# Loading ScalarE's sigmoid table first, spreading batch 1's folds one a step, and reordering the loads and the first products of a Fourier mixing and gated feed-forward kernel

## The chip, the cores and the metric

The kernel runs on one core of one Trainium2 chip. A core has a matrix engine (TensorE, PE in the profile, with its weight loads as PEld), a vector engine (VectorE, DVE), a scalar engine (ScalarE, ACT), a general engine (GpSimd, POOL), and SyncE (SP), which only issues DMAs here. Transfers run on 16 DMA engines that all queues share. SP, ACT and POOL each issue DMAs; the instructions of an engine, DMA issues among them, go in their order.

The metric is the device time in microseconds (us). The kernel before takes 1187.11 us, the median of three runs (1185.74 to 1187.33).

## The reference

```python
def _attn_ref(x):                        # x: 8 x 3136 x 256
    X = np.fft.fft(x, axis=1)
    X = np.fft.fft(X, axis=2)
    return X.real.astype(np.float32)

def _moe_ref(x, w_in, conv_w, w_out):    # 256 x 1024, 3 x 1024, 1024 x 256
    h = np.maximum(x @ w_in, 0.0)
    ...                                  # a zero row ahead of and behind h gives hp
    for k in range(3):
        conv_out += conv_w[k][None, None, :] * hp[:, k:k + S, :]
    gate = 1.0 / (1.0 + np.exp(-conv_out))
    return (h * gate @ w_out).astype(np.float32)
```

The second function is applied to the result of the first. The three weights arrive as 64-bit floats, `x` as 32-bit.

## The kernel before, in words

**Transform along the sequence.** For each of the 8 batches the kernel folds `x` by the symmetries of the transform. Two halves of `x` (`load_ops(b, 0, ...)` and `load_ops(b, 1, ...)`) come in, each as one plain load on SP and four mirrored gathers issued by POOL. `fold_ops(b)` gives eight operations for each half: two pair sums (`pair`), a difference and a sum (`both`), the odd features (`feats(1)`), `turned`, `evens`, and the even features (`feats(0)`). They are DVE work, with small POOL copies (`single`) and ScalarE scalings (`scaled`) beside them. For batch 0 `scaled` makes scaled copies (tiles `h`, called `parted`) and `turned` does nothing; for the other batches `turned` combines in place what `scaled` made.

`units(b)` then multiplies the folded rows by tables of cosines and sines. A unit is a group of matmuls, a copy on ScalarE and a finishing (`fin`) on DVE. There are four odd units (they use `tabs[1]`, the odd tables, of which half is mirrored by `mirror_tables` on ScalarE after `mend_row(1, ...)` halved one row) and four even ones (`tabs[0]`), and for batch 0 a small unit for one feature row. The finishings write the two matrices `qt` and `pt` (`PQ[b]`), 128 features x 1569 frequencies.

**Transform along the features, joined with w_in.** `blocks(i)` multiplies `dm`, the features' matrix, by a quarter of `w_in` and gives a quarter of `G`; `column(i)` gives one column of it, `ge`. `w_in` is narrowed from 64 to 32 bits by `narrow`: seven DVE operations, or, where a `room` is given, five on DVE and one on ScalarE. `taps` prepares the three convolution weights `cw`: one matmul, one ScalarE copy and six small DVE operations.

**The main loop.** A step is a batch, one of 4 chunks of frequencies, and one of 8 blocks of 128 of the 1024 hidden features: 256 steps, 32 a batch. `products` multiplies `G` with `qt` (PSUM tile `pb`) and with `pt` (`pa`, seeded by `seed`); `copies` takes `pb` out on ScalarE; `combine` adds both with a ReLU on DVE; `first_tap`, `middle` (an accumulating DMA) and `last_tap` are the convolution; `sigmoid` and `gate` follow four steps later; `mm2` multiplies by `w_out` five steps later and stores.

**What sets the order.** It is written out by hand. Ahead of the loop the program order is each engine's order: loads; the narrowing of the first weights and `taps`; all folds of batch 0; filler matmuls (`keep_on`) on PE while nothing else is ready; the odd units in four parts each (`part(i)`; parts 0 and 1 use x's first half, parts 2 and 3 its second); the feature unit and the even units; `column(0)`, `blocks(0)` and the narrowing of `w_in[1]`. In the loop, a table `side[(cycle, where)]` puts everything else at a step and at a place within the step: the narrowing of weights ("first" and "dve", steps 0 to 10), the folds and units of the next batch ("dve", "act", "pool", "pe"), and the loads ("load"). `ends[b]` is the step at which batch b's units begin; the folds of batch b lie between `ends[b-1]` and `ends[b]`, for batch 1 at the steps of a list.

Memsets of single elements by POOL (L118, L720 to L722) make the loads that write the same tile wait until POOL has issued its gathers. Lines that matter below: L157 to L228 folds, L261 to L280 tables, L288 `turn` (the factors of `scaled`), L296 and L302 mending and mirroring, L355 to L418 finishings, L619 to L637 narrowing, L698 to L706 `taps`, L740 and L750 copies of `G` and `ge`, L788 `copies`, L796 `combine`, L811 `last_tap`, L826 `sigmoid`, L835 `gate`. All matmuls have line L93, so PE's rows are told apart by their tiles.

## Time and profile before

| | us |
|---|---|
| median of the runs | 1187.11 (1185.74 to 1187.33) |
| profiled execution, its own time | 1188.7 |
| its span, first to last instruction | 1186.9 |
| busy: PE, DVE, ACT, POOL | 1144.0, 963.0, 945.9, 594.2 |
| PE weight loads | 890.8 |

The busy time is the time in which an engine had an instruction under way. A row of a timeline gives start, length, engine, line, operation, the tile written, the tiles read, shapes, how many instructions were merged, and in square brackets the idle time ahead of them on that engine with what ended it. A matmul of 32-bit floats stands as two instructions. A row of the groups gives the count, then busy us and mean ns of one, then idle us ahead with their releasers. An engine name with a q behind it is that engine's DMA issue.

### The profile page before, as it was taken

To read this page: it belongs to the slowest core of one execution; us is meant where nothing else is said; L and a number is where in the kernel's file an instruction comes from. 1 tells how busy PE (TensorE), PEld (TensorE's weight loads), DVE (VectorE), ACT (ScalarE), POOL (GpSimd) and SP (SyncE) were. 2 spreads that over 40 slices of the span, in tenths; PEclk is the share of its full clock that TensorE was granted. 3 is DMA by queue.
4 is the path that set the end of the run, shared out by engine and by line. 5 is a ranking of instruction groups with operands and counts; after the bars stand their busy time and mean duration, and the time that the engine had idled before them with its cause. 6 is when DMAs were issued, how large, how long until landed. Compare 5 with 4: busy or idle time off the path is not lost.

```text
span 1186.9 us, 16040 instructions
## 1 busy us (share of the span) xinstructions
PE 1144.0 (96%) x4818; PEld 890.8 (75%) x4818; DVE 963.0 (81%) x1448; ACT 945.9 (80%) x1939; POOL 594.2 (50%) x734
## 2 busy tenths in 40 slices
PE   4988999999999999999999999999999999999998
PEld 2755777777777787777777777777778777777777
DVE  7589988887888888988885887889788677788885
ACT  2488778787887888888887888888787788898884
POOL 5244745655374454556455464654444444444443
PEclk9899999999999999999999999999999999999999
DMA  8666696785677676867675576756565556666664
GB/s 206 191 99 145 152 166 147 156 174 119 136 170 160 129 157 143 169 134 170 143 162 131 94 175 143 170 128 130 117 125 117 115 122 139 131 134 124 129 119 98
DMA packets 107586, 168.15 MB, mean 142 GB/s; under 512 B 32657, under 2 KB 62627, under 8 KB 107501
## 3 DMA queue, kind: packets, MB, share of 16 engines
q0 software_dynamic: 41984, 115.83, 50.9%
q1 hardware_dynamic: 64345, 50.89, 15.1%
q8 instruction: 38, 0.62, 0.2%
q10 hardware_dynamic: 1172, 0.43, 0.2%
q14 instruction: 47, 0.39, 0.1%
HBM read 38.40 MB, written 25.74 MB: 54 GB/s over the span
## 4 chain that ended last, share of the span: by engine, by line
PE 70%; ACT 7%; DVE 6%; issue 3%; DMA 2%; POOL 2%; SPq 0%; ACTq 0%; DVEq 0%; POOLq 0%
PE po L93 44%; PE pb L93 11%; PE pa L93 10%; PE pd L93 5%; DVE g L811 2%; ACT g L826 2%; ACT nb L788 2%; ACT os L859 1%; DMA out_dram<-os 1%; POOL g L834 1%; DVE h L796 1%; DMA eb<-ed 1%; POOL xh L132 1%; ACT pa L767 1%; DMA xh<-in_x_dram 1%
## 5 line engine op out<-in xcount | busy, mean ns | idle before, releaser
L93 PE MATMUL po<-wout,g 128*128 128x256 f32 x3072 | 708.5, 380 | 10.3 <-DVE g L835 10.0
L93 PEld LDWEIGHTS po<-wout,g 128*128 128x128 f32 x3072 | 581.6, 190 | 157.8 <-DVE g L835 27.1
L806 POOL DMA_DIRECT2D g<-h x256 | 227.7, 889 | 481.5 <-ACT g L802 266.1
L826 ACT ACTIVATE g<-g,cw 128x385 f32<-128x385 f32 (+2 forms) x512 | 291.5, 621 | 77.7 <-DVE g L811 75.2
L834 POOL TENSOR_TENSOR g<-g,h 128x385 f32<-128x385 f32 (+1 forms) x256 | 287.6, 1124 | 56.9 <-ACT g L826 55.4
L788 ACT ACTIVATE nb<-pb 128x386 f32<-128x386 f32 (+3 forms) x512 | 226.1, 495 | 102.8 <-PE pb L93 101.0
L811 DVE SCALAR_TENSOR_TENSOR g<-h,cw,g 128x770 f32<-128x770 f32 (+1 forms) x256 | 288.1, 1125 | 0.0
L796 DVE CUSTOM_DVE_ANT_0 h<-pa,nb 128x386 f32<-128x386 f32 (+3 forms) x512 | 264.6, 557 | 28.4 <-POOL h L773 19.5
L802 ACT ACTIVATE g<-h,cw 128x770 f32<-128x770 f32 (+1 forms) x256 | 243.6, 952 | 0.0
L93 PE MATMUL pb<-qt,G 127*128 127x387 f32 (+2 forms) x512 | 214.5, 500 | 5.7 <-ACT nb L788 4.8
L93 PE MATMUL pa<-pt,G 128*128 128x387 f32 (+2 forms) x512 | 212.8, 496 | 0.5 <-ACT pa L767 0.4
L835 DVE TENSOR_TENSOR g<-g,h 128x385 f32<-128x385 f32 (+1 forms) x256 | 188.0, 734 | 25.3 <-ACT g L826 25.0
L767 ACT ACTIVATE pa<-eb,ge 128x387 f32<-128x387 f32 (+2 forms) x256 | 154.7, 604 | 3.2 <-DVE h L796 2.8
L93 PEld LDWEIGHTS pa<-pt,G 128*128 128x128 f32 x512 | 97.0, 190 | 75.0 <-issue 16.9
L93 PE MATMUL pd<-tab,w 98*128 98x197 f32 (+2 forms) x448 | 98.3, 318 | 3.1 <-DVE as L412 2.8
L132 POOL DMA_INDIRECT xh<-in_x_dram,idx x64 | 91.8, 1434 | 18.6 <-issue 11.5
L93 PEld LDWEIGHTS pb<-qt,G 127*128 127x128 f32 x512 | 90.8, 190 | 12.8 <-ACT nb L788 6.3
L93 PEld LDWEIGHTS pd<-tab,w 98*128 98x128 f32 (+1 forms) x448 | 81.9, 191 | 13.1 <-ACT pa L767 4.2
L859 ACT COPY os<-po 128x256 f32<-128x256 f32 x196 | 57.8, 390 | 14.5 <-DMA out_dram<-os 7.9
L157 DVE TENSOR_TENSOR xh<-xh 98x1020 f32<-98x1020 f32 (+1 forms) x32 | 47.8, 1497 | 0.0
L168 DVE TENSOR_TENSOR xh<-xh 98x1024 f32<-98x1024 f32 (+1 forms) x32 | 44.2, 1382 | 0.1
L194 DVE TENSOR_TENSOR w<-xh 98x508 f32<-98x508 f32 (+1 forms) x32 | 33.5, 1047 | 0.2
(140 smaller groups left out, 411.3 us busy)
## 6 DMA issues: line engine op xcount, KB each, us to landing
g<-h POOLq DMA_DIRECT2D x192, 385.0 KB, 4.0
g<-h POOLq DMA_DIRECT2D x64, 416.0 KB, 4.2
out_dram<-os SPq DMA_DIRECT2D x192, 128.0 KB
xh<-in_x_dram SPq DMA_DIRECT2D x16, 784.0 KB
eb<-ed SPq DMA_DIRECT2D x16, 193.5 KB
raw<-in_moe_w_in_dram SPq DMA_DIRECT2D x4, 512.0 KB
raw<-in_moe_w_out_dram SPq DMA_DIRECT2D x1, 2048.0 KB
eb<-ed SPq DMA_DIRECT2D x8, 209.0 KB
```

Source lines behind the costliest of these rows:

```text
L93: nc.tensor.matmul(o, l, r, start=start, stop=stop, skip_group_check=True)
L132: nc.gpsimd.indirect_dma_start(out=xh[b, h][0:NP, 7 - m].rearrange("p q d -> p (q d)"), out_offset=None, in_=bass.AP(tensor=x.tensor, offs ...
L767: act(pa[s][:, 0:n], eb[b, c], AF.Copy, scale=ge[:, f:f + 1])
L788: act(nb[s][:, i, cols], p[:, cols], AF.Copy, scale=-1.0 if i else 1.0)
L796: nc.vector._custom_dve(TENSOR_ADD_SAT, out=to, in0=a[:, cols], in1=c[:, i, cols], s0=BIG, s1=0.0)
L802: act(gs[s], hs[s][:, 0:n], AF.Copy, scale=cw[:, 0, s[2]:s[2] + 1])
L806: nc.gpsimd.dma_start(out=gs[s], in_=hs[s][:, 1:1 + n], accum_op=ALU.add)
L811: stt(out=g, in0=h[:, k:k + n], scalar=cw[:, k, f:f + 1], in1=g, op0=ALU.mult, op1=ALU.add)
L826: act(gs[s][:, c], gs[s][:, c], AF.Sigmoid, scale=cw[:, 1, s[2]:s[2] + 1])
L834: gt(g[:, p], g[:, p], h[:, p], op=ALU.mult)
L835: vt(g[:, v], g[:, v], h[:, v], op=ALU.mult)
L859: nc.scalar.copy(out=osb[:, j % 2], in_=pt[:, j % 2])
```

## The change

It does six things.

1. `act(first_use, low, AF.Sigmoid)` stands as ScalarE's first activation, behind one DMA issue.
2. Loads: the odd tables (`load_odd`, all on ScalarE's queue) and `dm` are issued ahead of x's second half as far as the program order goes; `turn` is issued by SP behind x's first half; the three `zero` loads by SP; the memset of the odd table's first elements goes, and another of its memsets goes in among POOL's first gathers.
3. Order ahead of the loop: mending and mirroring the odd tables come before the first folds on ScalarE; parts 0 and 1 of the odd units, `blocks(0)` and `column(0)` come between the two halves' folds; the filler is six matmuls behind them in place of eight ahead of everything; `taps` comes behind the second half's folds; the odd units' parts 2 and 3 go unit by unit; the narrowing of `w_in[1]` and `flip`, `store` and `spread` come after the third of the last five units.
4. In the loop the place "first" (where narrowings begin) moves from before to behind `products` and `copies`.
5. Batch 1: its 16 folds lie at steps 9, 11 to 14, 16, 16 and then 17 to 25 in place of 9 to 22 with four steps that had two; its units run in steps 22 to 29 in place of 21 to 28, odd units first. In every batch `scaled` comes one fold earlier.
6. Batch 2: folds from step 28 in place of 23, units from 45 in place of 44; batch 3's units from 70 in place of 68.

```diff
-            return ops, {3: single(1), 7: single(0)}, {5: scaled}
+            return ops, {3: single(1), 7: single(0)}, {4: scaled}
...
+    first_use = const.tile([P, 1], F32, name="first_use")
...
-    def taps():
-        p = spare()
+    def taps(bank):
+        p = bank()
...
     w_cv.load(nc.scalar)
+    act(first_use, low, AF.Sigmoid)
     w_in[0].load(nc.sync)
-    for f in load_ops(0, 0, nc.sync):
+    first = load_ops(0, 0, nc.sync)
+    for f in first[0:2]:
         f()
-    load_turn(nc.scalar)
-    for f in load_ops(0, 1, nc.sync, nc.scalar, True):
+    nc.gpsimd.memset(tabs[1][96:KR, 0:2, 0], 0.0)
+    for f in first[2:]:
         f()
-
+    load_turn(nc.sync)
+    load_odd(nc.scalar)
+    second = load_ops(0, 1, nc.sync, None, True)
+    second[0]()
+    nc.scalar.dma_start(out=dm, in_=dft_dim[:, :, 0:2])
+    for f in second[1:]:
+        f()
+    nc.gpsimd.memset(tabs[0][0:1, 0, 0, 0:1], 0.0)
+    load_even()
+    for i in (1, 2, 3):
+        w_in[i].load(nc.sync)
     w_cv.narrow(0, 1)
     w_in[0].narrow(0, 2)
-    taps()
-    act(turn[0:NP, 2], turn[0:NP, 1], AF.Copy, scale=-1.0)
-    nc.gpsimd.memset(tabs[0][0:1, 0, 0, 0:1], 0.0)
-    nc.gpsimd.memset(tabs[1][0:1, 0:2, 0, 0:1], 0.0)
-    nc.gpsimd.memset(tabs[1][96:KR, 0:2, 0], 0.0)
-    load_even()
-    load_odd(nc.sync, 0)
-    load_odd(nc.scalar, 1)
-    nc.sync.dma_start(out=dm, in_=dft_dim[:, :, 0:2])
-    for i in (1, 2, 3):
-        w_in[i].load(nc.sync)
...
-    for j, f in enumerate(ops):
-        if j in pres:
-            pres[j]()
-        f()
-
-    odds = [us[j] for j in (0, 1, 5, 6)]
-    keep_on([idle] * 6)
-
-    keep_on([psa.tile([P, 512], F32, name="pa", tag="pa") for _ in range(2)])
+    act(turn[0:NP, 2], turn[0:NP, 1], AF.Copy, scale=-1.0)
+
+    def folds(h):
+        n = len(ops) // 2
+        for j in range(n * h, n * h + n):
+            if j in pres:
+                pres[j]()
+            ops[j]()
+
     mend_row(1, half)
     mirror_tables()
-    mend_row(0, half)
-    for i in range(4):
-        for j, u in enumerate(odds):
+    folds(0)
+    for i in range(2):
+        for u in odds:
             u.part(i)
-            if i == 3:
-                u.copy()
-                u.fin()
...
+    blocks(0, bank_a)
+    column(0, bank_b)
+    keep_on([bank_b()] * 4)
+    keep_on([bank_a() for _ in range(2)])
+    folds(1)
+    taps(bank_b)
+    for j, u in enumerate(odds):
+        u.part(2)
+        u.part(3)
+        u.copy()
+        u.fin()
+        if j == 1:
+            mend_row(0, half)
+            row()
...
     for i, u in enumerate(us[j] for j in (4, 2, 3, 7, 8)):
         u.matmuls(0, 1)
         u.copy()
         u.fin()
-        if i == 0:
+        if i == 2:
             flip()
             store()
             spread(0, range(1, len(chunks)))
+            for f in w_in[1].parts(0, 2, room):
+                f()
...
-    column(0)
     for f in load_ops(1, 0, nc.sync):
         f()
-    blocks(0)
-    room = left[:, NF // 2:].rearrange("p f i -> p (f i)").bitcast(I32)
-    for f in w_in[1].parts(0, 2, room):
-        f()
...
-    ends = [9, 23, per + 12] + [per * (b - 1) - 3 + max(11 - 4 * (b - 2), 0) for b in range(3, B)]
+    ends = [9, 25, per + 13, 2 * per + 6][0:B] + [per * (b - 1) - 3 + max(11 - 4 * (b - 2), 0) for b in range(4, B)]
...
-        us = us[0:4] + us[5:]
-
-        c0 = ends[b] - 2 * (b == 1)
-        n = per * b - 3 - c0
+        us = us[0:2] + us[5:7] + us[2:4] + us[7:] if b == 1 else us[0:4] + us[5:]
+
+        c0 = ends[b] - 3 * (b == 1)
+        n = per * b - (2 if b == 1 else 3) - c0
...
-            cs = [9, 11, 11, 12, 12, 13, 14, 14, 16, 17, 17, 18, 19, 20, 21, 22]
+            cs = [9, 11, 12, 13, 14, 16, *range(16, 26)]
...
+            if b == 2:
+                c0, n = c0 + 3, n - 3
             cs = [free(c0 + j * n // len(ops)) for j in range(len(ops))]
...
-        run("first")
         if t + 1 < n:
             products(steps[t + 1])
             copies(steps[t + 1])
+        run("first")
         run("act")
```

`load_odd` keeps its transfers but issues both parts of a parity one behind the other, the 48-partition pieces first, then the last two rows and the extra row. `blocks` and `column` take the PSUM bank as an argument; `bank_a` and `bank_b` hand out the banks that the loop's `pa` and `pb` use.

More of the change, by code (lines that the diff above doesn't have):

```diff
@@ L731, with blocks @@
     ge = const.tile([P, NF], F32, name="ge")
-    def blocks(i):
+    def blocks(i, bank=spare):
         w = w4[i]
         for g in range(2):
-            p = spare()
+            p = bank()
             for t in range(2):
@@ L742, in blocks, with column @@
             column(i)
-    def column(i):
-        w, p = w4[i], spare()
+    def column(i, bank=spare):
+        w, p = w4[i], bank()
         for m in range(NF // 4):
@@ L862, in mm2, with bank_a, bank_b @@
         gs.pop(s)
-    idle = psb.tile([P, 512], F32, name="pb", tag="pb")
+    def bank_a():
+        return psa.tile([P, 512], F32, name="pa", tag="pa")
+    def bank_b():
+        return psb.tile([P, 512], F32, name="pb", tag="pb")
     def keep_on(banks):
@@ L871, in keep_on @@
                True, True)
+    room = left[:, NF // 2:].rearrange("p f i -> p (f i)").bitcast(I32)
     begin, us, row, flip, store = units(0)
@@ L876 @@
     nc.gpsimd.memset(PQ[0][1][96:P, :], 0.0)
+    odds = [us[j] for j in (0, 1, 5, 6)]
     ops, _, pres = fold_ops(0)
[L878 to L886 removed]
+    act(turn[0:NP, 2], turn[0:NP, 1], AF.Copy, scale=-1.0)
[5 more added lines that the diff above has]
+            ops[j]()
     mend_row(1, half)
     mirror_tables()
[L889 to L891 removed]
+    folds(0)
+    for i in range(2):
+        for u in odds:
             u.part(i)
[L893 to L900 removed]
+    blocks(0, bank_a)
[12 more added lines that the diff above has]
+            row()
+            w_out = Weight(wout, moe_w_out.rearrange("(c p) o -> p c o", p=P),
+                           lambda sh: xp.tile(sh, I32, name="raw", tag="xh"))
+            w_out.load(nc.sync)
     for i, u in enumerate(us[j] for j in (4, 2, 3, 7, 8)):
```

26 lines of the change are left out of this document (11 added, 15 removed).

## The prediction

> **What bounds the kernel now.** I read the page first (busy shares, the 40 slices), then the busy time by stretches, then the timeline of the first 110 us, the groups of DVE's lines and the DMA queue's waits.
>
> ```profile
> PE 1144.0 (96%) x4818; PEld 890.8 (75%) x4818; DVE 963.0 (81%) x1448; ACT 945.9 (80%) x1939; POOL 594.2 (50%) x734
> ...
> PE   4988999999999999999999999999999999999998
> DVE  7589988887888888988885887889788677788885
> ...
> PEclk9899999999999999999999999999999999999999
> ```
>
> TensorE (PE) is busy 1144.0 of 1186.9 us, and in the slices it is a wall of nines from the sixth on. So a change elsewhere counts only where PE now stands still or runs slowly: 42.9 us in all. The stretches show where. I cut them at events of the timeline: step 0's first product (49.4), and those of step 9 (86.31), step 26 (169.96) and step 32, batch 1's first (198.99).
>
> ```profile
> 0.00:28.20 28.20, 11.95 (x30) 6.37 (x30) 22.07 (x40) 5.35 (x13) 15.58 (x33) 1.00 0.82 204
> ...
> 49.40:71.40 22.00, 17.28 (x73) 11.35 (x73) 15.59 (x30) 18.45 (x39) 5.03 (x9) 1.00 0.95 151
> ...
> 86.31:169.96 83.65, 76.76 (x320) 56.89 (x319) 76.18 (x116) 64.90 (x145) 45.88 (x51) 1.00 0.77 148
> 169.96:198.99 29.03, 29.03 (x129) 23.22 (x129) 25.14 (x45) 23.66 (x49) 15.71 (x18) 1.00 0.74 172
> ```
>
> Columns: length, then busy us (instructions) of PE, PEld, DVE, ACT, POOL, then granted clock, DMA share, GB/s. Before 28.20 PE lacks 16.3 us (and most of its 12 busy us are filler, below). In 86.31:169.96, steps 9 to 25, it lacks 6.9 us. From 169.96 it lacks nothing: there PE alone sets the pace.
>
> **Part 1: the time to the first step.** Here are the rows that set PE's path from the first data to step 0.
>
> ```profile
> 11.28 0.17 DVE L700 TENSOR_TENSOR small<-cw 128x8 f32<-128x8 f32 x1 [1.95 <-ACT cw L698]
> 12.28 2.35 DVE L157 TENSOR_TENSOR xh<-xh 98x1020 f32<-98x1020 f32 x2
> 16.72 0.63 POOL L200 TENSOR_TENSOR w<-xh,sg 98x4 f32<-98x4 f32 x1
> 16.84 7.60 PE L93 MATMUL pb<-w 98*128 98x512 f32 x12 [11.24 <-POOL w L179]
> 17.57 0.62 ACTq L280 DMA_DIRECT2D tab<-dft_seq_dram  x1
> 18.29 1.71 ACT L218 ACTIVATE h<-w,turn 98x256 f32<-98x256 f32 x4 [6.94 <-DMA xh<-in_x_dram]
> 24.28 1.88 PE L93 MATMUL pa<-w 98*128 98x512 f32 x4
> 26.00 0.49 PE L93 MATMUL po<-tab,w 98*128 98x196 f32 x2
> 27.83 0.80 ACT L296 ACTIVATE tab<-tab,half 2x196 f32<-2x196 f32 x2
> 29.91 0.60 PE L93 MATMUL po<-tab,w 98*128 98x196 f32 x2 [1.68 <-ACT tab L302]
> 37.12 0.86 PE L93 MATMUL po<-tab,h 98*128 98x197 f32 x4
> 38.72 4.85 PE L93 MATMUL po<-tab,w 99*128 99x99 f32 x32
> 42.59 0.36 DVE L355 TENSOR_TENSOR as<-as,po 128x197 f32<-128x197 f32 x1 [1.32 <-ACT as L351]
> 45.30 3.60 PE L93 MATMUL po<-win,dm 128*128 128x256 f32 x8
> 45.47 0.56 DVE L369 TENSOR_TENSOR pt<-as,po 128x392 f32<-128x392 f32 x1
> 48.94 0.43 DVE L619 TENSOR_SCALAR win<-raw 128x512 int32<-128x512 int32 x1 [2.91 <-issue]
> 50.65 0.92 PE L93 MATMUL pa<-pt,G 128*128 128x386 f32 x2 [0.37 <-ACT pa L767]
> 51.07 0.69 DVE L637 SCALAR_TENSOR_TENSOR win<-raw,win 128x512 f32<-128x512 f32 x1
> 54.17 1.89 PE L93 MATMUL po<-win,dm 128*128 128x256 f32 x8
> ```
>
> Folds of x's first half begin at 12.28, one after `taps` (released by ACT at 11.28), and run unbroken on DVE to about 29.8, both halves. The filler (512 columns, 12 instructions from 16.84) starts at half speed: 7.60 us for 12, against 1.88 for 4 later, so 0.47 us each warm; at twice 0.43 for the slow ones the slow start lasts 4.5 to 5 us. The odd units' 48 instructions run from 26.00 to 37.98; less the 1.68 us wait for the mirrored table (29.91) and 1.71 us of slow clock (below) that is 8.6 us, 0.18 each.
>
> Removed and moved, one by one. `taps` leaves the head of DVE: its idle 1.95 and six small operations go, up to 3.0 us (from 9.33, 11.28 less its idle, to 12.28). Against that x's first half gets company on the DMA engines: the odd tables, seven issues on ACT now ahead of x's second half, and `turn`, four issues moved to SP behind x's first load and in front of its second.
>
> ```profile
> 10.00:20.00 10.00, 3.16 (x4) 1.51 (x5) 8.45 (x16) 3.04 (x7) 5.61 (x11) 1.00 1.03 241
> SPq L266 <- DMA tab<-dft_seq_dram: 5.7, 1, 5.7
> ```
>
> The engines are full there (1.03), so what goes in front delays what is behind. All four odd-table pieces are 294 KB by their shapes (96 partitions x 4 runs x 784 B), some 1.2 us at 241 GB/s and more if short rows are slow; the features' matrix `dm`, 262 KB, another 1.1 us for the second half. Also an issue can wait for an earlier transfer to land (5.7 us for L266), and everything behind it on that queue waits too: on ACT that is the table scaling, the mirroring and `scaled`, on SP x's second half and the even tables. Bounds for the first folds: 3.0 us earlier to 1.2 us later. I take no change, since lost and won are alike; they end at 29.8 as now. Neither end is on PE's path in what follows, for the filler covers it.
>
> PE now starts with real work: parts 0 and 1 of the odd units (24 instructions) when `scaled` of the first half is there, 17.6 (POOL's last operation for it ends at 17.35; now ACT begins at 18.29, behind the DMA issue of 17.57). Cold for 4.9 us, 13 instructions at twice 0.18; the other 11 take 2.0: 24.5. `blocks(0)` 1.9 (54.17's row; the 3.60 at 45.30 was half speed), `column(0)` 1.0, its copy 0.3: 27.7. Then six fillers of two instructions, 5.6 us: 33.3; `taps`' product 0.3: 33.6. The second half's products could start at about 27.8 (its `scaled` ends there today, ahead of 27.83's row), so the filler, not x, is last there, and x may come 5 us later at no cost. Parts 2 and 3, 24 x 0.18 = 4.4: 38.0, the same end as today's 37.98. Features and evens follow in 5.6 us (37.98 to 43.57): 43.6.
>
> What is gained is behind it: `column(0)` and `blocks(0)`, which end at 48.90 today, no longer stand in front of step 0. What comes in their place is DVE. The narrowing of `w_in[1]` (48.94 to 51.76, 2.8 us) is moved in front of the last two even units' finishing, which makes `pt`. An even pair is finished by two operations of 0.36 and two of 0.56 (42.59, 45.47), 1.8 us; so is an odd pair's last. Last odd product 38.0, ACT's copy 0.4, finishing 1.8: 40.2; first even pair, copy 0.4 and 1.8: 42.4 (`flip` on ACT no longer in between); narrowing 2.8: 45.2; second even pair: 47.0, and 0.3 for handing over. Today `pt` is ready at 46.03. So step 0's `pa` product starts at 47.4 instead of 50.65: **3.25 us gained**. From below: today's 46.03 and the narrowing, 48.9, 1.8 gained; from above, no filler on the path and DVE as early, 46.0, 4.6 gained. I take the value between them that the order gives; it is nearer the row that it starts from, the odd products' end, which doesn't move.
>
> One price is open: evens to 43.6, the row product and `pb` of 0.9 each to 45.4, then PE idles until 47.4. The clock falls after such idle:
>
> ```profile
> 30.00:35.00 5.00, 5.00 (x20) 5.00 (x21) 0.00 (x0) 1.00 (x2) 0.00 (x0) 0.66 0.62 206
> ```
>
> Its share was 0.66 there. A dip costs what `blocks(0)` lost, 3.60 - 1.89 = 1.7 us. Idle of 1.68 (29.91) came before this one; I leave a dip out of the sum and keep it in the range. [...]
>
> **Part 2: ScalarE's table.** The sigmoid's table is loaded in the middle of the ramp, and the narrowing's ACT operation stands in front of step 5's copies.
>
> ```profile
> 67.48 1.28 ACT L826 ACT_TABLE_LOAD   x1
> ...
> 68.77 1.12 ACT L826 ACTIVATE g<-g,cw 128x385 f32<-128x385 f32 x2
> ...
> 69.80 0.70 ACT L621 ACTIVATE wout<-wout,low 128x512 int32<-128x512 int32 x1
> 70.42 0.84 ACT L788 ACTIVATE nb<-pb 128x385 f32<-128x385 f32 x2
> ...
> 71.31 0.92 PE L93 MATMUL pb<-qt,G 127*128 127x386 f32 x2 [2.64 <-ACT nb L788]
> ...
> 73.42 4.07 PE L93 MATMUL po<-wout,g 128*128 128x256 f32 x12 [0.30 <-DVE g L835]
> ...
> 78.63 2.75 PE L93 MATMUL po<-wout,g 128*128 128x256 f32 x12
> ```
>
> PE waits 2.64 us for those copies and then runs slow: 4.07 us for 12 products against 2.75. With a sigmoid first in the kernel the first load brings the sigmoid's table; after 67.48 no load follows, though copies and ReLU run between sigmoids, so that one load serves all. So 1.28 goes, and 0.70 goes behind the copies ("first" moved): step 6's `pb` starts 1.95 earlier, idle 0.7, too short for a dip. But step 0's output products still wait for DVE's gate. DVE waits for the moved ACT operation: it ends 0.3 to 0.4 earlier than today, and the gate 0.5. So the 12 products start at 72.9, 0.5 earlier, and take 1.3 less without the dip: **1.8 gained** (0.5 if the dip stays, 1.95 + 1.3 = 3.3 at best). The load itself costs 1.28 us at the start, ahead of the odd tables' issues; ACT has nothing else to do there. [...]
>
> **Part 3: batch 1's folds, steps 9 to 25.**
>
> ```profile
> L157 DVE TENSOR_TENSOR xh<-xh 98x1020 f32<-98x1020 f32 (+1 forms) x6 | 9.3, 1555 | 0.0
> L228 DVE SCALAR_TENSOR_TENSOR w<-w,turn,rt 98x256 f32<-98x256 f32 x4 | 3.1, 813 | 3.7 <-POOL g L834 2.3 <-ACT rt L222 1.4
> ```
>
> PE's 6.9 idle us lie in front of output products and copies while DVE is at 76.2 of 83.65, full but for 7.5 us, of which 3.7 are in front of `turned` (L228), waiting for POOL and for ACT's `scaled` of the same step. After: one operation a step up to step 25, `scaled` one operation earlier, so the 3.7 go. The work in these 17 steps shrinks: batch 2's first folds (two pair sums, 2 x 1.2 of L157's 9.3) leave for step 28, and PE passes one unit, 1.4 us, to step 29. DVE is left with 73.8, PE with 75.4: PE is the longer one. From 83.65 the least is 75.4; the unit comes back later, so 6.9 at most. Products of batch 1 then have one step less between their last unit (finished in step 30) and step 32; PE needs 29.03 / 6 = 4.8 us a step there, DVE's finishing 1.1, and DVE is busy 25.1 of those 29.0: no wait. I take that 2.0 us of idle remain, from latencies as in steps 0 to 8: **4.9 gained**; bounds 0 (PE's idle only moves) and 6.9.
>
> **Part 4: batch 2.** Its folds run in steps 28 to 44 instead of 23 to 43, one a step.
>
> ```profile
> 198.99:255.00 56.01, 55.02 (x228) 41.06 (x227) 49.36 (x74) 46.67 (x97) 34.62 (x46) 1.00 0.68 141
> ```
>
> DVE has 6.6 us free in these 56, and 3.9 in the 29 before. Five operations at about 1.2 to 1.5, some 6.5 us, are pushed into it. **0.5 lost**, from nothing to 3.0. The new waits behind it (x of batch 2 loaded three steps later, the row spread one step later) have 10 us of steps in front of their users.
>
> **Sum.** The profiled execution took 1188.7 (span 1186.9): 1188.7 - 3.25 - 1.8 - 4.9 + 0.5 = 1179.25. The median of the runs, 1187.11, is 0.13% under the profiled one: **1177.7**.
>
> **The rivals.** (a) The head gains nothing: tables in 784-byte rows and ACT's issues shift all by what `blocks(0)` saves. For it: the full DMA engines; against: 5 us of filler. 1177.7 + 3.25 = 1181.0. (b) The folds' idle only moves, since DVE stays full: 1177.7 + 4.9 = 1182.6. For it: DVE's two nines in the slices (89 to 148 us); against: 3.7 us of its waits that go. (c) More than forecast: all idle of part 3 and the upper end of part 1: 1177.7 - 2.0 - 1.4 = 1174.3, 1173 with a part of the 4.7 us that PE still lacks in 49.4 to 71.4.
> (d) Slower: the odd tables land late. They now stand first on PE's path: mending and mirroring (2.0 us, ACT) come before `scaled`. If they land at T, PE's chain starts at T + 2.5 instead of 17.6, as much later is step 0. In the trace they had landed by 27.83, where ACT takes them up. With T = 15.1 my sum holds; at T = 24.6 all 9.45 us are gone; above 27.0 it is slower by over 0.2%; at 27.8 it is 1177.7 + 12.7 = 1190.4. Against it: seven issues of 0.6 us (17.57's row) behind the table's load end near 9 if none waits. For it: the full engines, and waits like L266's 5.7.
> (e) The table's load doesn't go (a second one in the loop stays): 1179.5.
>
> **How the numbers follow.** Forecast 0.50, (a) 0.13, (b) 0.10, (c) 0.11, (d) 0.15, of which 0.09 lands above +0.2% and 0.06 around no change, (e) 0.01. A 0.2%, 2.4 us, is about what can be told from no change. Faster 0.85, same 0.06, slower 0.09. The range takes in the forecast with a clock dip and with (a) and (b), and most of (c): 1172 to 1184; (d) is left out.
>
> **What would show it.** One ACT_TABLE_LOAD, before 4 us; step 0's `pa` at about 47.4, waiting for DVE's `pt`; `blocks(0)` at 1.9 us; step 7 at some 72.5; DVE's idle in front of L228's successor near nothing; step 9 to 26 in 77 to 78 us; batch 1's first product some 9 us before 198.99. Wrong, if ACT's mirroring ends after 20, if the clock dips in steps 0 to 3, or if PE idles in steps 28 to 44.

## The result, and the profile after

The changed kernel takes 1189.45 us (median of nine runs, 1186.98 to 1192.21), the kernel before 1185.98 in its nine (1182.79 to 1188.59). The ratio is 1.0029, with a 95% interval of 1.0015 to 1.0043: slower by 0.3%, where 0.8% faster was predicted. The profiled execution took 1192.21 us, its span is 1190.4, 3.5 more than before's 1186.9. That execution is the slowest of the nine.

Of the page of the changed kernel, the busy times and slices that answer to those shown before:

```profile
PE 1141.6 (96%) x4814; PEld 890.8 (75%) x4814; DVE 969.9 (81%) x1448; ACT 943.2 (79%) x1939; POOL 611.3 (51%) x733
...
PE   0988999999999999999998999999999999999998
...
PEclk9999999999999999999999999999999999999999
```

PE is busy 2.4 us less than before, and the whole is 3.5 us longer. The first slice has gone from 4 to 0: PE starts later. The starts of the steps (first `pb` product of each) in the two timelines say where the time went; the forecast of the head was made for `pa`, which came 6.97 us later:

| stretch | before, us | after, us | difference | predicted |
|---|---|---|---|---|
| start to step 0 | 49.37 | 55.44 | +6.07 | -3.25 (to `pa`) |
| steps 0 to 4 | 17.75 | 19.72 | +1.97 | 0 |
| steps 5 to 8 | 19.19 | 18.51 | -0.68 | -1.8 |
| steps 9 to 31 | 112.68 | 107.78 | -4.90 | -4.9 |
| step 32 to the end | 987.9 | 989.0 | +1.05 | +0.5 |
| sum | 1186.9 | 1190.4 | +3.5 | -9.45 |

So the folds of batch 1 did what was forecast, the table gave a good third of its term, and the head, in place of giving 3.25 us, took 6. PE's timeline of the changed kernel in that stretch (start, length, operation, tiles, shapes, count, idle ahead and what ended it):

```profile
19.65 0.99 PE L93 MATMUL po<-tab,w 98*128 98x196 f32 x2 [19.65 <-DMA tab<-dft_seq_dram]
28.88 1.65 PE L93 MATMUL po<-tab,h 98*128 98x197 f32 x4 [8.24 <-DMA tab<-dft_seq_dram]
...
34.91 1.31 PE L93 MATMUL po<-tab,h 98*128 98x197 f32 x4
36.06 1.89 PE L93 MATMUL pa<-win,dm 128*128 128x256 f32 x8
...
38.99 3.70 PE L93 MATMUL pb<-w 98*128 98x512 f32 x8 [0.25 <-ACT ge L753]
42.53 1.88 PE L93 MATMUL pa<-w 98*128 98x512 f32 x4
44.34 0.40 PE L93 MATMUL pb<-ident,cw 24*128 24x24 f32 x2
...
49.81 4.85 PE L93 MATMUL po<-tab,w 99*128 99x99 f32 x32
54.59 0.91 PE L93 MATMUL pd<-er,one 1*128 1x386 f32 x2
55.44 0.92 PE L93 MATMUL pb<-qt,G 127*128 127x386 f32 x2
57.62 0.89 PE L93 MATMUL pa<-pt,G 128*128 128x386 f32 x2 [1.27 <-ACT nb L791]
```

PE begins at 19.65 with one odd product, and its second one, which multiplies `tab` by `h`, then waits 8.24 us for a table's transfer. From 28.88 on it stands only 0.25 us until `pa`: odd parts 0 and 1, `blocks(0)`, and the filler as well (38.99 to 44.4), which is now in the middle of the path. What it waited for is seen in SP's timeline of the same kernel (each row a DMA issue):

```profile
13.94 5.51 SPq L126 DMA_DIRECT2D xh<-in_x_dram  x2
19.61 1.36 SPq L261 DMA_DIRECT2D tab<-dft_seq_dram  x2
21.02 0.44 SPq L263 DMA_DIRECT2D tab<-dft_seq_dram  x1
21.51 0.64 SPq L266 DMA_DIRECT2D tab<-dft_seq_dram  x1
```

These are the even tables (L261 to L266, `load_even`), not the odd ones. Two of their pieces are 589.5 KB each. The odd tables had landed by some 20 us: ScalarE mends and mirrors them from 18.53 on, in its timeline:

```profile
18.53 0.45 ACT L297 ACTIVATE tab<-tab,half 2x196 f32<-2x196 f32 x1 [5.46 <-DMA tab<-dft_seq_dram]
...
20.27 1.17 ACT L303 ACTIVATE tab<-tab 99x196 f32<-99x196 f32 x4 [0.28 <-DMA tab<-dft_seq_dram]
21.35 1.69 ACT L218 ACTIVATE h<-w,turn 98x256 f32<-98x256 f32 x4
```

The code says why an odd unit waits for the even tables. The description above has all four odd units on `tabs[1]`. But `product` takes its table from `tabs[0]` for `st` 0 and 1 and from `tabs[1]` for 2 to 5, and two of the four odd units, those of `odd(sn)`, loop over `i` in 0 and 1 and pass `i` as `st`:

```
            mms = [product((slice(0, P), slice(i * n, (i + 1) * n)), from_(i, e), i, q,
                           slice(0, HE, 2), i + q + e == 0, q == 2 and e == m - 1)
                   for q in (0, 2) for i in range(2) for e in range(m)]
```

The kernel before issued the even tables first (L266's issue at 21.96 is the last of them) and the odd ones behind. Each order makes one pair of the odd units wait for the tables that come last; before, that was the 1.68 us at 29.91.

The gain of part 3 stands in the stretches of the changed kernel, cut at 93.67 (step 9), 171.40 (step 26) and 201.45 (step 32):

```profile
93.67:171.40 77.73, 74.99 (x311) 56.01 (x310) 72.67 (x109) 63.93 (x144) 51.06 (x49) 1.00 0.81 150
171.40:201.45 30.05, 30.05 (x139) 24.15 (x138) 25.57 (x45) 23.10 (x48) 12.98 (x16) 1.00 0.78 180
```

PE's missing time in steps 9 to 25 is 2.74 us, where it was 6.89; steps 26 to 31, to which one unit moved, take 1.02 us more. The groups of DVE in the first of them show the wait in front of `turned` gone:

```profile
L228 DVE SCALAR_TENSOR_TENSOR w<-w,turn,rt 98x256 f32<-98x256 f32 x4 | 4.2, 1091 | 0.0
```

### The profile page after: what moved, and what is told of

Read it like the earlier page. It is cut to its first block, busy times and chain, and to the rows that moved or that the text cites. A ratio compares the mean times of both kernels' runs of the same rounds, so it can differ in the third digit from the quotient of the medians.

```text
span 1190.4 us, 16050 instructions
## 1 busy us (share of the span) xinstructions
PE 1141.6 (96%) x4814; PEld 890.8 (75%) x4814; DVE 969.9 (81%) x1448; ACT 943.2 (79%) x1939; POOL 611.3 (51%) x733
## 4 chain that ended last, share of the span: by engine, by line
PE 77%; ACT 4%; DVE 3%; issue 1%; DMA 1%; POOL 0%; ACTq 0%; DVEq 0%; SPq 0%
PE po L93 48%; PE pb L93 12%; PE pa L93 11%; PE pd L93 6%; ACT nb L791 1%; ACT g L829 1%; ACT os L862 1%; DVE g L814 1%; DMA out_dram<-os 1%; ACT g L805 0%; ACT pa L770 0%; DVE g L838 0%; DVE h L799 0%; DVE w L228 0%; DVE pt L419 0%
## 5 line engine op out<-in xcount | busy, mean ns | idle before, releaser
L837 POOL TENSOR_TENSOR g<-g,h 128x385 f32<-128x385 f32 (+1 forms) x256 | 305.8, 1195 | 56.5 <-ACT g L829 54.9
L814 DVE SCALAR_TENSOR_TENSOR g<-h,cw,g 128x770 f32<-128x770 f32 (+1 forms) x256 | 282.9, 1105 | 0.0
L157 DVE TENSOR_TENSOR xh<-xh 98x1020 f32<-98x1020 f32 (+1 forms) x32 | 44.8, 1403 | 2.7 <-DMA xh<-in_x_dram,idx 2.0
L168 DVE TENSOR_TENSOR xh<-xh 98x1024 f32<-98x1024 f32 (+1 forms) x32 | 46.7, 1459 | 0.1
L386 DVE TENSOR_TENSOR as<-as,pd 128x196 f32<-128x196 f32 x14 | 5.0, 358 | 37.7 <-ACT as L382 37.7
```

Of the source, the lines that this page charges most:

```text
L814: stt(out=g, in0=h[:, k:k + n], scalar=cw[:, k, f:f + 1], in1=g, op0=ALU.mult, op1=ALU.add)
L837: gt(g[:, p], g[:, p], h[:, p], op=ALU.mult)
```

## The experiments

The theory: the even tables' landing at 28.9 sets when PE starts, and everything that PE does before step 0, the filler too, lies behind it. Rivals: the landing is late only because its issue waits for other transfers (the 5.51 us at 13.94 hold back L261); the filler is hidden in some other wait; the loss is in the loop. Medians, each beside runs of the kernel before on the same chip. The ratio is estimated from all of the runs and can differ a little from the quotient of the medians. The changed kernel itself ran again beside e14 to e16 (e13); where another run is set against its 1189.45, the two were not measured side by side.

| run | edit | median, us | before, us | ratio (95%) |
|---|---|---|---|---|
| e1 | even tables issued earlier | 1189.76 | 1186.73 | 1.002 (1.001 to 1.003) |
| e2 | no filler | 1181.21 | 1186.73 | 0.995 (0.9935 to 0.9965) |
| e3 | loop alone | 1180.55 | 1186.73 | 0.9943 (0.9927 to 0.9958) |
| e4 | early table, "first" moved | 1186.54 | 1186.73 | 0.9993 (0.9982 to 1.0004) |
| e5 | e3 and e4 | 1180.06 | 1186.08 | 0.9947 (0.9928 to 0.9966) |
| e6 | head with early table, old loop | 1190.79 | 1186.08 | 1.0038 (1.0025 to 1.0051) |
| e7 | filler ahead of the odd units | 1184.83 | 1186.08 | 0.9984 (0.9965 to 1.0003) |
| e8 | filler and `blocks(0)` ahead | 1180.96 | 1186.08 | 0.9965 (0.9952 to 0.9978) |
| e9 | e8, narrowing later | 1179.90 | 1186.23 | 0.9947 (0.9934 to 0.9961) |
| e10 | even tables ahead of x's second half | 1186.16 | 1186.23 | 1.0001 (0.9991 to 1.0011) |
| e11 | `dm` behind the even tables | 1188.77 | 1186.23 | 1.0023 (1.0012 to 1.0034) |
| e12 | filler doubled | 1194.33 | 1186.23 | 1.0078 (1.0063 to 1.0094) |
| e13 | the changed kernel again | 1189.89 | 1187.54 | 1.0021 (1.0006 to 1.0037) |
| e14 | e6 again | 1190.44 | 1187.54 | 1.003 (1.0016 to 1.0044) |
| e15 | e5 again | 1179.89 | 1187.54 | 0.9936 (0.9912 to 0.996) |
| e16 | e9, two fillers less | 1177.66 | 1187.54 | 0.992 (0.9898 to 0.9943) |

The filler's results are never used, so the kernels with more or less of it compute the same.

**What makes the tables late: e1, e10, e11.** In e1 the three `zero` loads go from SP to POOL, so the even tables' issues don't stand behind them.

```diff
-    second = load_ops(0, 1, nc.sync, None, True)
+    second = load_ops(0, 1, nc.sync, nc.gpsimd, True)
...
-    for f in second[1:]:
+    for f in second[2:]:
...
     load_even()
+    second[1]()
```

> The changed kernel, but the three one-row loads of x's second half (the zero loads) are issued by GpSimd behind its gathers, so that they no longer stand on SyncE's queue ahead of the even tables. Theory: the odd units read the even tables too; these were issued only at 19.61 us, behind a zero load that waited until 18.82 for an odd-table piece to land, and PE stood still until 28.88. Then the even tables are issued near 13 us, PE's second product starts at 21 to 24 instead of 28.88, step 0 comes 4 to 7 us earlier than at 55.44, and the time is 1182 to 1186. Rival (the filler and the cold clock set the head): PE's second product is earlier, step 0 moves by less than 1.5 us, time 1188 to 1190.

In e1's timeline of SP and PE the first three issues stood 4.7 us earlier; the wait on PE ended where it had:

```profile
14.89 1.33 SPq L261 DMA_DIRECT2D tab<-dft_seq_dram  x2
16.27 0.43 SPq L263 DMA_DIRECT2D tab<-dft_seq_dram  x1
20.35 0.67 SPq L266 DMA_DIRECT2D tab<-dft_seq_dram  x1
...
28.72 1.65 PE L93 MATMUL po<-tab,h 98*128 98x197 f32 x4 [8.51 <-DMA tab<-dft_seq_dram]
```

The last piece (L266, one row) was issued only 1.2 us earlier, but little can hang on it. The even tables are the only transfers here in packets of 6,288 bytes, 198 of them, 192 in the two big pieces. They run from 21.06 to 27.31 us in the changed kernel's trace and from 16.99 to 27.71 in e1's, and the 192nd to end does so at 26.36 and 26.31. So the big pieces start 4.1 us earlier and end no earlier. The rival falls: the time of the issue isn't the cause. In the changed kernel the DMA engines' share is 0.95 from 10 to 20 us and 0.89 from there to 28.88. e11 takes 256 KB (`dm`) out from in front of the even tables:

```diff
-    nc.scalar.dma_start(out=dm, in_=dft_dim[:, :, 0:2])
...
     load_even()
+    nc.sync.dma_start(out=dm, in_=dft_dim[:, :, 0:2])
```

> The changed kernel with dm issued by SyncE behind the even tables, as before, instead of by ScalarE ahead of x's second half. Theory (the DMA engines are full to 28 us, so what goes in front delays the even tables by its volume): 0.26 MB less in front, the even tables land about 1.1 us earlier, PE's second product at 27.6 to 28.0, step 0 at 54.2 to 54.8, time 1188 to 1189. Rival (the order of issue and its waits decide): no change or, if dm is then late for blocks(0), 1 us slower.

From PE's timeline of e11:

```profile
27.07 1.65 PE L93 MATMUL po<-tab,h 98*128 98x197 f32 x4 [6.48 <-DMA tab<-dft_seq_dram]
```

The second product started 1.8 us earlier, and step 0 at 53.42, 2.0 earlier. In the other traces with these loads in this order that product starts at 28.1 to 29.6, so e11's lies 1.1 us below the earliest of them; 256 KB take 1.2 us at the 210 GB/s of this stretch. The median, 0.7 lower, can't be told from the changed kernel's. e10 issues the even tables in front of x's second half:

```diff
     load_odd(nc.scalar)
+    load_even()
     second = load_ops(0, 1, nc.sync, None, True)
...
-    load_even()
```

(The one-element memset that held their issue back is left out too.)

> The changed kernel with the even tables issued on SyncE right ahead of x's second half; filler and all else as in the change. Theory (the odd units need the even tables, which came behind x's second half, and this is the root): PE's second product starts at 19 to 22 instead of 28.88, the filler lies in the wait for x's second half, step 0 starts at 45 to 48 instead of 55.4, time 1180 to 1183. Rival (the 1.2 MB only change places, x's second half comes 5 us later and parts 2 and 3 wait for it behind cold products and filler): step 0 at 50 to 54, time 1185 to 1188.

PE's timeline of e10:

```profile
22.98 0.99 PE L93 MATMUL po<-tab,w 98*128 98x196 f32 x2 [22.98 <-DMA tab<-dft_seq_dram]
25.76 1.68 PE L93 MATMUL po<-tab,h 98*128 98x197 f32 x4 [1.79 <-ACT h L218]
...
38.31 1.88 PE L93 MATMUL pa<-w 98*128 98x512 f32 x4
```

Now the even tables land at 22 to 24 us, and the odd ones, sharing the engines with them (share 0.88 from 0 to 23 us), at 21 to 23; mirroring and `scaled` follow. PE goes on 3.1 us earlier than in the changed kernel, and the median is 3.3 lower. It is level with before, not better, because the filler still stands on the path (34.77 to 40.1). So what counts is the volume that must have landed before the first odd unit can run: both tables and x's first half.

**The filler: e2, e12, e7.** e2 leaves the six filler matmuls out, e12 doubles them, e7 puts them ahead of the odd units.

```diff
-    keep_on([bank_b()] * 4)
-    keep_on([bank_a() for _ in range(2)])
```

> The changed kernel without its six filler matmuls. They run from 38.99 to 44.41; the second half's scaled copies end at 40.56. If late tables alone make the loss and the filler is only in the way behind them, step 0 comes 3.5 to 4.5 us earlier and the time is near 1185.5. If the filler is needed for the clock, a stretch at half speed appears ahead of 55 us and less than 2 us are gained. If the filler costs nothing (PE waits for something else behind it), step 0 stays at 55.4 and the time at 1189.5.

> The changed kernel with twice the filler (twelve instead of six matmuls) at the same place. Theory (all of the filler is on PE's path there): 12 more instructions of 0.45 us, step 0 5.4 us later, near 60.8, time 1194 to 1196. Rival (filler partly hidden in a wait behind it): less than 3 us.

> The changed kernel with its six filler matmuls moved ahead of the odd units' parts 0 and 1, into the time in which PE waits for the even tables; nothing else moved. Theory (filler on the path and a cold start behind the wait): odd parts run at 0.18 us an instruction instead of 0.33, filler is hidden, step 0 at 46 to 48 instead of 55.4, time 1180 to 1182.5; no slow clock ahead of step 0. Rival (only the late tables count): step 0 at 49 as without filler, time as there, 1181; the difference from it, if any, is the clock: there 6.8 us at half speed from 51.6.

Of e2, from PE's timeline:

```profile
36.79 0.95 PE L93 MATMUL pb<-dm,win 128*128 128x1 f32 x8
37.98 0.40 PE L93 MATMUL pb<-ident,cw 24*128 24x24 f32 x2 [0.25 <-ACT ge L753]
...
49.34 0.92 PE L93 MATMUL pb<-qt,G 127*128 127x386 f32 x2
```

And of e12:

```profile
37.66 7.13 PE L93 MATMUL pb<-w 98*128 98x512 f32 x16 [0.25 <-ACT ge L753]
44.63 3.60 PE L93 MATMUL pa<-w 98*128 98x512 f32 x8
...
59.25 0.92 PE L93 MATMUL pb<-qt,G 127*128 127x386 f32 x2
```

Without the filler `taps`' product follows the column at once. Step 0 starts 6.1 us earlier than in the changed kernel, but 1.0 of this was there before the column. From the column's start to step 0 it is 12.55 us for 17.65, so the filler cost 5.1. Doubled, it runs from 37.66 to 48.2; step 0 starts only 3.8 later, as the column ended 1.3 earlier in that trace. From the filler's start to step 0 it is 21.59 us for 16.45, again 5.1. Both directions agree: the filler of the change covers next to nothing and costs 5.1 of the 5.4 us that it lasts. The medians, 8.2 lower and 4.9 higher, hold other things too: e2's trace also takes 5.2 us less than the changed kernel's in steps 133 to 159 (below), and its slow clock behind step 0 lasts twice as long (6.8 us from 51.6, against 3.41 from 59.76). Ahead of the odd units (e7) the filler fills the wait in part, from 17.89 to 25.6; PE then still stands 2.50 us until 28.46, and the clock falls twice, at 29.4 (the products' rows of 0.86 us take 1.52) and for 6.8 us at 49.9 (1.49 for 0.81). Step 0 starts at 48.23, earlier than in e2, but the median gains only 4.6 against the changed kernel, and 1180 to 1182.5 was expected. Steps 133 to 159 take 121.1 us in its trace, for 116.7 in e2's.

**The order: e8, e9, e16.** In e8 `blocks(0)` and `column(0)`, which need neither table, stand in the wait with four fillers on each side, and the odd units behind. e9 also puts `w_in[1]`'s narrowing back behind step 0's products (in the changed kernel the `pt` of step 0's `pa` stands behind it) and `column(1)` behind step 1's. e16 is e9 with two fillers less. e8's edit:

```diff
     folds(0)
+    keep_on([bank_b()] * 4)
+    blocks(0, bank_a)
+    column(0, bank_b)
+    keep_on([bank_b()] * 4)
     for i in range(2):
         for u in odds:
             u.part(i)
-    blocks(0, bank_a)
-    column(0, bank_b)
-    keep_on([bank_b()] * 4)
-    keep_on([bank_a() for _ in range(2)])
```

> The changed kernel with filler (four), blocks(0), column(0) and filler (four) in front of the odd units' parts 0 and 1, all in the wait for the even tables; the filler behind them is gone. Theory: blocks(0) and column(0), 2.9 us, leave PE's path too, but pt is then last: step 0's pb at 44 to 46, its pa at 46.5 to 48.5 waiting for DVE, time 1178 to 1181. Rival: the even tables land later than PE's filler ends and nothing more is gained than with the filler first: within 1 us of that run.

> The run with blocks(0), column(0) and filler in front of the odd parts, with one more edit: the narrowing of w_in[1] goes behind step 0's products and copies, and column(1) behind step 1's products. Theory: step 0's pa waited 1.26 us for pt, whose finishing stood behind that narrowing on DVE, and the idle brought 3.4 us of half clock at 48.0. Then pa follows pb within 1 us, no slow stretch falls into steps 0 to 3, and it is 2 to 3 us faster than that run (1180.96): 1178 to 1179. Rival: DVE's combine of step 0 is now behind the narrowing, step 2 starts no earlier than 52.8, same time within 1 us.

> Blocks and column first, narrowing later, with two instead of four fillers between column(0) and the odd units (1.85 us less by the 3.70 us of four). If this filler sets when the odd units start: 1.8 us better than with four, 1178. If the even tables' landing at 28 to 29 us sets it: 0 to 0.8 better, and an idle on TensorE stands in front of the first odd product that reads them, with a chance of a clock dip that costs 1.7.

In e8 the odd units run without a wait from 28.39, step 0 starts at 43.69, and `pa` waits 1.26 us. PE's timeline of e16:

```profile
18.03 5.67 PE L93 MATMUL pb<-w 98*128 98x512 f32 x8 [18.03 <-POOL w L179]
23.54 1.89 PE L93 MATMUL pa<-win,dm 128*128 128x256 f32 x8
...
26.46 1.99 PE L93 MATMUL pb<-w 98*128 98x512 f32 x4 [0.25 <-ACT ge L753]
28.28 0.50 PE L93 MATMUL po<-tab,w 98*128 98x196 f32 x2
28.61 0.88 PE L93 MATMUL po<-tab,h 98*128 98x197 f32 x4
...
43.60 0.92 PE L93 MATMUL pb<-qt,G 127*128 127x386 f32 x2
44.87 0.92 PE L93 MATMUL pa<-pt,G 128*128 128x386 f32 x2 [0.35 <-ACT pa L770]
```

The four products at 28.61 take 0.88, where the same ones took 1.65 in the changed kernel at 28.88: the slow start is spent on filler (5.67 us for eight, 3.70 in the changed kernel). There is no wait in front of the tables' products, so the remaining filler was what set their start in e9 (30.41 there), and step 0 begins 2.1 us earlier than in e9. `pa` waits 0.35, not 1.27. e16 is 0.8% faster than the kernel before, the fastest of all, 12.2 us under the changed kernel run beside it. Of its 9.9 us, the new loop with the early table gives 7.65 behind the old head (e15, run beside it), so the mended head is worth about 2.2; the two intervals overlap. From e8 to e9 step 0's `pa` waits 0.9 us less, and the median fell by 1.1, where 2 to 3 was expected; that difference was not measured side by side.

**The parts alone: e3 to e6.** e3 is the kernel before with the folds and units of parts 5 and 6 of the change; e4 has only the sigmoid at the start and the moved "first"; e5 has both; e6 is the changed kernel with the old folds, units and place of "first". Of the edits, the list of folds in e3 and the two of e4:

```diff
-            cs = [9, 11, 11, 12, 12, 13, 14, 14, 16, 17, 17, 18, 19, 20, 21, 22]
+            cs = [9, 11, 12, 13, 14, 16, *range(16, 26)]
...
+    act(first_use, low, AF.Sigmoid)
...
-        run("first")
         if t + 1 < n:
             products(steps[t + 1])
             copies(steps[t + 1])
+        run("first")
```

> The kernel before with the change's order of batch 1's and 2's folds and units alone; head, table load and narrowing as before. Theory: from step 9 to step 32 it takes 4.9 us less (as 112.7 became 107.8), and about 1 us is lost behind it: 3.9 us faster than before, near 1182. Rival: the 4.9 came from the later and slacker start of that kernel's loop; then steps 9 to 32 take 111 to 113 us and the time is within 1.5 us of the kernel before.

> The kernel before with the sigmoid's table loaded first, and the place where narrowings begin moved behind products and copies; nothing else. Theory: steps 5 to 7 take 1.9 us less (8.3 instead of 10.2), and step 8 gives back about 1.2 because DVE's narrowing is then behind ScalarE's: 0.5 to 1 us faster, 1185 to 1185.5. Rival A (step 8's loss belongs to something else): 1.9 faster, 1184. Rival B (all of it hidden): no change.

> The head of the kernel before, with the change's loop (folds, units) and its early table load and later narrowing. The loop alone was 6.2 us faster (1180.55 against 1186.73), the table alone 0.2. Theory (both act, in different steps): 6 to 8 us faster, about 1179 to 1180.5. Rival (the narrowing behind ScalarE's copies costs DVE in step 8 what the table gives): the same as the loop alone or up to 1.5 us more.

> The changed head and the early table load with the loop of the kernel before. Theory: the whole loss is in the head, so step 0 starts near 55 and steps 9 to 32 take 112 to 113 us again: 6 to 10 us slower than the kernel before, 1193 to 1197. Rival (head and loop hide each other's times): 1189 to 1191, as the whole change.

Steps 9 to 31 take 107.7 us in e3 and 107.8 in e5, 112.6 in e6: the 4.9 us are the loop's, behind either head. Steps 32 to 132 take 1.3 us less too: 440.8 in e3 and e5, where before, e4 and e6 have 442.1 to 442.2. The two make e3's 6.2, where 3.9 was expected. (In e4 steps 9 to 31 take 110.1, so its table and "first" shift some of this too, and against e4 the loop brings only 2.3 there; why wasn't looked into.) e4's gain is not told from zero. e6 is 4.7 us slower than before, where 6 to 10 was expected: step 0 is late as expected (54.96), but its trace takes 1.3 less in steps 5 to 8 and 2.9 less in steps 133 to 159. Steps 5 to 8 take 19.2 us before, 19.2 in e3, 18.5 in e4, 18.5 after and in e15, and 17.9 in e6, which has the early table with "first" at its old place. So in the traces the early table is worth 1.3 us, and moving "first" costs 0.6 of it. The slow clock that stood in this place in before is worth nothing there: e3, with the table's load where it was, has no such dip and is not shorter. Its output products of steps 0 and 2 in PE's timeline,

```profile
70.10 2.86 PE L93 MATMUL po<-wout,g 128*128 128x256 f32 x12 [0.54 <-DVE g L835]
...
80.28 2.86 PE L93 MATMUL po<-wout,g 128*128 128x256 f32 x12 [1.79 <-DVE g L835]
```

and the second of them before (the first, 4.07 us long at 73.42, is shown above),

```profile
83.62 2.86 PE L93 MATMUL po<-wout,g 128*128 128x256 f32 x12 [0.93 <-DVE g L835]
```

and both in the changed kernel:

```profile
80.80 2.86 PE L93 MATMUL po<-wout,g 128*128 128x256 f32 x12 [1.46 <-DVE g L838]
...
90.98 2.86 PE L93 MATMUL po<-wout,g 128*128 128x256 f32 x12 [1.97 <-DVE g L838]
```

What the products save, PE waits longer for DVE's gate: 1.79 and 1.97 us against 0.93. It is the gate that ends the wait in these steps, and a faster PE only waits longer for it.

**Do the parts add? e13 to e15.** The head alone lost 4.7 us, the loop with the table gained 6.0, and together 3.5 were lost. The three were run side by side.

> The changed kernel again, beside its two halves. If the parts add, it stands at the head's loss plus the loop's gain (about 1185 if those are +4.7 and -6.0); if they don't, at about 1189.5 as before, and the trace then shows where behind step 32 it loses what the loop with the table alone doesn't lose.

> The changed head with the early table load, the old loop. Theory that the head costs what its first step is late (6 us in the profile against the before's profiled execution, 9 to 10 against an execution without a clock dip in the head): 1192 to 1196. Theory that separate comparisons were right: 1190.8.

> The old head, the early table load and the new loop. Both theories: 1180, between 1179 and 1181.5. The difference to the changed kernel is the new head's price behind the new loop: 9.4 us if the earlier medians hold, 4.7 if the head alone measures it right.

They don't add: +2.9 and -7.65 make -4.75, and +2.35 was measured. The new head costs 10.0 us behind the new loop (e13 against e15; 8.8 at step 0 in their traces, 55.32 against 46.48) and 2.9 behind the old one. Of these 7.1 us, 1.3 are the early table's, which e14 has and before has not (steps 5 to 8). Another part is seen at step 134, where PE waits for the finishing of batch 5's odd unit. PE's timeline of e13:

```profile
652.35 0.44 PE L93 MATMUL pd<-tab,w 99*128 99x99 f32 x2 [2.50 <-DVE as L413]
```

and e14:

```profile
654.66 0.44 PE L93 MATMUL pd<-tab,w 99*128 99x99 f32 x2 [0.38 <-DVE as L413]
657.04 2.86 PE L93 MATMUL po<-wout,g 128*128 128x256 f32 x12 [0.63 <-DVE g L838]
```

With the new head and the old loop these waits are 1.0 us, in e6 too, and also in e2 and e12, which have the new loop. In all other traces the first of them is 2.5 to 3.8, and in all but e16 a slow clock follows (from 630 to 670 us the granted clock is 0.91 in the changed kernel, 0.96 in before, e9, e13 and e15, 1.00 in e16). Steps 133 to 159 take 116.7 us in the four traces with the short wait and 119.0 to 122.1 in the others; the changed kernel has 121.95 and e13, the same kernel, 119.63. So neither the head nor the loop alone decides it. e14 takes 2.9 us less there than before (116.73 for 119.64). In the changed kernel ScalarE stands 4.3 us there for a store's transfer. That leaves some 3 us of the 7 that single traces can't place; what decides how long this wait is stays open. No run tried more buffers for the stores.

## Why the prediction was wrong

**The step that failed** is the one that begins "PE now starts with real work: parts 0 and 1 of the odd units (24 instructions) when `scaled` of the first half is there, 17.6". It left out that the units of `odd(sn)` read `tabs[0]`, the even tables, whose issue the change had put behind the odd ones and x's second half. The start was 28.88, not 17.6. What followed on PE up to the evens was right: forecast for the ends of odd parts, column, filler, parts 2 and 3 and evens were 24.5, 27.7, 33.3, 38.0 and 43.6; measured are 36.1, 39.0, 44.4, 49.0 and 54.6, all later by 11.0 to 11.6. `pa` came at 57.62 for 47.4, which turns the 3.25 us that it was to gain into 6.97 lost. e1, e10 and e11 show that it was the tables' landing, and that what had to land first set it.

**"Then six fillers of two instructions, 5.6 us: 33.3".** The forecast had these on PE's path too. What was too small is the price of keeping them: "no filler on the path and DVE as early" was to bring `pa` from 47.4 to 46.0, 1.4 us, but it is 5.1 (e2, e12), because DVE's finishings wait for the odd and even products and come earlier with them. The cover named for them, a late second half of x, was not needed: its folds ended at 29.90, as forecast (29.8), and its scaled copies at 40.56, 1.6 us behind the filler's start.

**Rival (d)** had the mechanism and put it on the wrong tables. The odd ones' mirroring ended at 21.44, past the 20 that the prediction named as a sign of failure, but the even tables came last. Its formula, with 11.3 us in place of its delay, gives 1177.7 + 11.3 = 1189.0; measured 1189.45. That it comes so near is partly luck: the dip and part 2 each cost 1.1 us more than the sum has; against that, `pa` was 10.2 later than forecast and not 11.3, and the kernel before was 1.1 lower in its nine runs than in the three that the sum starts from. The chance of 0.09 for it was too low: the prediction never looked up which table the `po<-tab,h` products read, and the trace of before didn't show it, since the even tables were issued first there.

**The clock dip,** left out of the sum and priced at 1.7 us, came. In the changed kernel it follows 57.62's idle of 1.27 us; its stretch, with the granted clock third from the end:

```profile
59.80:63.21 3.41, 3.41 (x8) 2.23 (x7) 2.94 (x7) 2.81 (x5) 0.00 (x0) 0.51 0.61 169
```

Half the clock for 3.41 us is 1.7 us of PE's work. Steps 0 to 4 lost 1.97; in e13, the same kernel without a dip, they lost 0.89, so the dip cost 1.1. The idle itself was forecast: `pt` behind the narrowing.

**Part 2:** one ACT_TABLE_LOAD was left, at 1.44 us, and step 6's `pb` waits 0.62, for the 0.7 forecast. The step that failed is "and take 1.3 less without the dip": the dip went, and 1.0 of it went into the wait for DVE's gate two steps later (1.97 for 0.93). 0.68 was gained over steps 5 to 8, for 1.8; without the moved "first" it would have been 1.3 by e6.

**Part 3:** right, in size (4.9) and place: `turned`'s idle at 0.0, steps 9 to 25 in 77.7 us as forecast (77 to 78).

**Part 4:** 0.5 lost was forecast, 1.05 measured from step 32 on, and that it looks near is luck. Steps 32 to 132 take 1.3 us less, with this loop in every trace but e1's (0.8), as a wait of 1.48 us at 372.4 in before is gone: the part had the wrong sign. The other +2.3 lie in steps 133 to 159, outside what the part named, and e13, the same kernel, has none of them (119.63 us, before 119.64).

**The base.** The profiled execution of before has more slow clock in its head than others of the same head (0.50 from 31.54 to 34.95 us and from 45.19 to 48.60, where `blocks(0)` took 3.60 us for 1.97 in e3): step 0 starts at 49.37 there, at 46.05 in e3, which has the same head, and at 45.0 to 46.6 in e4, e5 and e15, which add the early table to it. A forecast of the head from one execution carries 3 to 4 us of this, as much as was forecast for it.

## What to carry to other kernels

When work is moved to the front, list for each of its instructions every tensor that it reads and when the last of them lands, from the code and not from the unit's name. Where the DMA engines were full (share 0.89 to 0.95), an issue 4.7 us earlier brought nothing (e1); the volume that must land first set the start, and work that needs none of it belongs into the wait (e16). Filler in front of the wait cost nothing where the wait outlasted it (by 2.50 us in e7) and also spent the slow start (e16); behind the wait it cost 5.1 of its 5.4 us.

## What the runs showed of the hardware that was not expected

- The granted clock falls to half (0.51 in 59.80:63.21 of the changed kernel) for 3.41 us, for 6.83 in some executions (from 653.68 in the changed kernel). It did so after PE had waited for 1.26 us (e8) to 3.59 (the changed kernel, step 134), and not each time: the same 1.27 us in front of step 0's `pa` was followed by it in the changed kernel and e6, not in e13 and e14, which are the same two kernels. Steps 0 to 4 took 19.72 and 19.73 us with it, 18.64 and 18.04 without. In before it also fell at 45.19 (0.50 to 48.60), though PE's rows show no wait since the 1.68 us at 29.91. The changes of the clock lie whole multiples of 3.413 us apart (in the changed kernel 23.89, 3.41 and 590.51 us, 7, 1 and 173 times; in before 10.24, 23.89 and 576.85, 3, 7 and 169 times).
- Where the idle in front of `pa` begins between two such points may decide, by the author's estimate from these traces: 0.0 to 0.5 us behind one the clock fell (the changed kernel, e1, e6, e8, e11), 0.9 to 1.2 behind it did not (e10, e13, e14). No run tested this, and later positions went both ways (e2 and e7, e12).
- After the 8.24 us of idle PE's products took nearly twice their time from 28.88 to 35.9, about 7 us (rows of 1.52 us, 0.86 in e16). The prediction had counted 4.9 us for such a start, from the kernel before. The stretches show a granted clock of 1.00 there, but the trace has no record of the clock ahead of 35.87, where the slow rows end, and what isn't recorded is counted as full: the rows show the slow start, the clock column doesn't. From PE's first product behind its long idle to the first such record it is 4.0 us in e16, 4.5 in before, 5.3 in e13 and 7.0 in the changed kernel.
- Moving the start of the loop changed a wait 600 us later (0.4 to 3.8 us at step 134): parts that are measured apart need not add.
